# Expert stages in two arms with tighter capacities, their order written out for five engines

## The chip, the core and the metric

The kernel runs on one core of one Trainium2 chip. A core has TensorE (matmuls, with the load of the stationary operand shown as PEld), VectorE (DVE), ScalarE (ACT), GpSimd (POOL) and SyncE (SP), which here issues most of the DMAs. Each engine has its own instruction queue, and they wait for each other by semaphores. The metric is the device time of one execution in microseconds; lower is better.

## The reference, cut to what matters

```python
attn_out = _attn_ref(q, k, v, n_global, n_local)      # 2 batches, 8 heads, 768 x 64, a local window and global columns
x = attn_out.transpose(0, 2, 1, 3).reshape(1536, 512)
x = _moe_ref(x, w_in, w_out)                          # h = x @ w_in; g = h * tanh(softplus(h)); g @ w_out
# routed experts, N, D, E, F = 1536, 512, 8, 1024
logits = x @ w_gate
expert_idx = argmax(logits, axis=1)
for e in range(E):
    mask = expert_idx == e
    h = maximum(x[mask] @ w1[e], 0)
    out[mask] = gate_w[mask, None] * (h @ w2[e])
```

Each token goes to the one expert of its largest logit. How many tokens an expert gets is known only when the kernel runs.

## The kernel before, in words

The kernel has three parts. Attention and the dense layer take about the first 365 us. They write the tokens that leave the dense layer to a buffer `xg` in DRAM, each behind the others of its expert, by an indirect DMA. Then `final_rank` orders the experts by their number of tokens, and the rest of the kernel works through them from the fullest to the emptiest. This third part is what the change touches.

The work of the third part is cut into nine stages, listed in `STG`. A stage is a rank, an offset and a fixed number of token columns, its capacity: stage 0 has the first 160 tokens of the fullest expert (`EARLY`), stage 1 the rest of its capacity of 336, so 176, and stages 2 to 8 have one expert each with the capacities 288, 256, 224, 208, 200, 184 and 176 (`CAPS`). Columns behind the last token of an expert hold zeros and an invalid row number. If an expert has more tokens than the capacity of its rank, a flag makes a slow path behind the stages run.

A stage has eight steps m. In step m, `b_L1(g, m)` multiplies the tokens by 128 columns of the first weight matrix, in four accumulating matmul groups; two steps later (`LAG`) `b_L2(g, m)` multiplies the result by 128 rows of the second, into four accumulators `bacc`. float32 values are split into a high and a low part in the fp32r format, and three products are summed (`mm3`). Below 256 columns the high and the low part of the tokens lie side by side and one matmul of twice the width does two of the products (`cat`): a pair of matmuls a group. From 256 columns on it is three matmuls. So a stage has 64 pairs or 64 triples: 32 in `b_L1`, 32 in `b_L2`.

The other engines work beside these matmuls:

- The weights of the next expert come in eight loads of 512 KB (`b_raw`, on SyncE's queue, six buffers). Each is split in two halves by a cast on ScalarE (L160) and a subtraction on VectorE (L161): 16 casts and 16 subtractions an expert (`b_conv`).
- The result of a `b_L1` of fewer than 256 columns is copied by ScalarE (L768), added by VectorE (L769), activated by ScalarE (L776), and VectorE makes its low part (L777). From 256 columns on only the last two are there.
- The token rows of the next stage are loaded (`b_xload`), transposed on TensorE 128 at a time (L721), and split by ScalarE (L726) and VectorE (L727), in `b_xprep`, at step 5.
- When a stage's last `b_L2` is done, `b_yevac` takes the four accumulators out (ScalarE L809, VectorE L810); then `b_yout` transposes them back (L824), scales them (L826, VectorE) and scatters them to the output by GpSimd (L828), 128 tokens at a time.

The order of the first part is written out by hand. The order in each engine's queue in the third part is a scheduler's, which goes by the order of the program text and by its own estimate of when things are ready, over all stages and the early one at once. At the very end each engine loads a flag (L1148) and branches over the slow path (L1149).

Of the kernel before, what the change touches and what calls it, by code (L numbers as in the profile page):

```python
# [8 lines left out]
F32 = mybir.dt.float32  # L9
# [23 lines left out]
CAPS = [336, 288, 256, 224, 208, 200, 184, 176]  # L33
CAPMAX = max(CAPS)
# [9 lines left out]
def moe_kernel(ctx, tc, q, k, v, n_global, n_local, w_in, w_out, w_gate, w1, w2, out, dbg=None):  # L44
# [608 lines left out]
    STG = [(0, 0, EARLY), (0, EARLY, CAPS[0] - EARLY)] + [(r, 0, CAPS[r]) for r in range(1, NE)]  # L653
# [8 lines left out]
    braw = {}  # L662
    bx = {}
# [6 lines left out]
    def b_raw(r, i):  # L670
        which, f, kk = CH[i]
        er = ereg[r]
        if r == 0:
            if kk == 0:
                w0f[which, f] = wp.tile([128, 4, 512], F32, tag="w", name="w0f")
            st = w0f[which, f][:, 2 * kk:2 * kk + 2, :]
        else:
            st = stp.tile([128, 2, 512], F32, tag="st", name="bst")
# [6 lines left out]
    def b_conv(r, i):  # L685
        which, f, kk = CH[i]
        if kk == 0:
            pool, tag = (wp, "w") if nsw[0] % 6 != 3 else (wlate[0], "w2")
            nsw[0] += 1
            sw[r, which, f] = [pool.tile([128, 4, 512], F32R, tag=tag, name="bw") for _ in range(2)]  # L690
# [6 lines left out]
    def b_xload(g):  # L697
# [3 lines left out]
        for i in range(nt):  # L701
            n = min(128, cap - i * 128)
            xr = xe.tile([128, ROW], F32, tag="x2", name="xr")
# [8 lines left out]
    def b_xprep(g):  # L712
        cap = STG[g][2]
        bp = bpool[0]
        meta = bp.tile([128, 3, 2], F32, tag="meta", name="meta", bufs=4)
        idi = bp.tile([128, 3], I32, tag="idi", name="idi", bufs=4)
        xc = bp.tile([128, 4, 2, cap] if g else [128, 4, cap], F32R if g else F32, tag="xc", name="xc")
        for i, (xr, n) in enumerate(bx[g]):
            tp = ps.tile([128, 4, 128], F32, tag="b", name="btp")
# [10 lines left out]
        bx[g] = (meta, idi, xc)  # L730
# [14 lines left out]
    def b_L1(g, m):  # L745
# [3 lines left out]
        hp = ps.tile([128, 512], F32, tag="b", name="bhp")  # L749
# [8 lines left out]
        wh, wl = sw[r, 1, m // 4]  # L758
        cs = slice((m % 4) * 128, (m % 4) * 128 + 128)
        for kk in range(4):  # L760
            mm3(hp, cap, cat, wh[:, kk, cs], wl[:, kk, cs], xc[:, kk, 0, :], xc[:, kk, 1, :],
                xc[:, kk].rearrange("p a c -> p (a c)"), kk == 0, kk == 3)
        if cat:
            hc = wk.tile([128, 2, cap], F32R, tag="gh", name="hc", bufs=3)
            hh, hl = hc[:, 0], hc[:, 1]
            hc = hc.rearrange("p a c -> p (a c)")
            t1 = wk.tile([128, cap], F32, tag="e", name="t1")
            nc.scalar.copy(t1, hp[:, cap:2 * cap])  # L768
            nc.vector.tensor_add(t1, t1, hp[:, 0:cap])  # L769
            src = t1  # L770
        else:
            hc = None
            hh = wk.tile([128, cap], F32R, tag="gh", name="hh", bufs=3)
            hl = wk.tile([128, cap], F32R, tag="gl", name="hl", bufs=3)
            src = hp[:, 0:cap]
        nc.scalar.activation(out=hh, in_=src, func=AF.Relu)  # L776
        ins = nc.vector.scalar_tensor_tensor(out=hl, in0=src, scalar=0.0, in1=hh.bitcast(F32),  # L777
                                             op0=ALU.max, op1=ALU.subtract)
        if g == 1:
            hlast[m] = ins.ins  # L780
        hcs[g, m] = (hh, hl, hc)

    def b_L2(g, m):
        r, _, cap = STG[g]
        cat = cap < 256
        if m == 0:
            bacc[g] = [ps.tile([128, 512], F32, tag="b", name="bacc") for _ in range(4)]
# [12 lines left out]
    yss = {}  # L800

    def b_yevac(g):
        cap = STG[g][2]
        acc = bacc.pop(g)
        yss[g] = [wk.tile([128, cap], F32, tag="n" if d < 2 else "r", name="ys") for d in range(4)]
        for d in range(4):
            ys = yss[g][d]
# [8 lines left out]
    def b_yout(g):  # L816
        cap = STG[g][2]
        meta, idi, _ = bx.pop(g)
        ys = yss.pop(g)
        for i in range((cap + 127) // 128):  # L820
            n = min(128, cap - i * 128)
            tp = ps.tile([128, 512], F32, tag="b", name="ytp")
            for d in range(4):
                nc.tensor.transpose(tp[0:n, d * 128:(d + 1) * 128], ys[d][:, i * 128:i * 128 + n], ident)  # L824
            yo = wk.tile([128, DM], F32, tag="cv", name="yo")
            nc.vector.tensor_scalar(out=yo[0:n], in0=tp[0:n, :], scalar1=meta[0:n, i, 1:2], scalar2=None,  # L826
                                    op0=ALU.mult)
# [145 lines left out]
    bpool[0] = main.enter_context(tc.tile_pool(name="bp", bufs=2, side="right"))  # L973
# [70 lines left out]
    def final_rank():  # L1044
# [16 lines left out]
        capr = const.tile([1, NE], F32, name="capr")  # L1061
        for r in range(NE):
            nc.gpsimd.memset(capr[:, r:r + 1], float(CAPS[r]))
# [7 lines left out]
        flagf = const.tile([1, 2], F32, name="flagf")  # L1071
# [4 lines left out]
        flag = const.tile([1, 2], I32, name="flag")  # L1076
# [9 lines left out]
    def early_block():  # L1086
# [19 lines left out]
        b_yevac(0)  # L1106

    early_block()
    for i in range(8, NM + YLAG + 1):
        g, m = divmod(i, 8)  # L1110
        if i < NM:
            r = STG[g][0]
            b_L1(g, m)
            if m == 0 and g > 1 and g + 1 < len(STG):
                b_reg(r + 1)
            if m == 0 and g + 1 < len(STG):
                b_xload(g + 1)
            if m == 5 and g + 1 < len(STG):
                b_xprep(g + 1)
# [241 lines left out]
```

## Time and profile before

| | us |
|---|---|
| median of 3 runs | 578.6 |
| lowest and highest of them | 577.35 to 579.09 |
| profiled execution, its own time | 578.08 |
| its span, first to last instruction | 576.4 |

The profiled execution is 0.1% below the median. The span is what the trace covers; the execution's own time has 1.7 us around it. The granted TensorE clock is 0.996 of full speed over the span. Engines run side by side, so their busy times don't add up to the span.

### The profile page before, as it was taken

The numbers are of one execution on the slowest core, as the hardware profiler recorded it, in microseconds if no ns is written. First come the engines' busy times: TensorE is split into PE (matmuls) and PEld (weight loads), VectorE is DVE, ScalarE is ACT, GpSimd is POOL, SyncE is SP. The second block draws the span as 40 slices with busy tenths as digits, with TensorE's granted clock in tenths as the row PEclk, the third lists the DMA queues.
The fourth block names the chain that finished last, engine by engine and source line by source line (L and its number), as shares of the span: only waits on it lengthen the run. The fifth ranks groups of instructions, "written<-read, shape, count | busy, mean of one in ns | idle before, by whom it ended". The sixth has DMA issues, their size and how long they took to land.

```text
span 576.4 us, 12667 instructions
## 1 busy us (share of the span) xinstructions
PE 560.0 (97%) x4650; PEld 517.7 (90%) x4650; DVE 470.0 (82%) x1142; ACT 379.6 (66%) x890; POOL 82.6 (14%) x155
## 2 busy tenths in 40 slices
PE   8999999999999999999999999899999999999993
PEld 6898989988999898989898988699999999999993
DVE  7899999899999997687776868486966687988842
ACT  7999899795767676456565555366645466777631
POOL 3113010010000100101011111041121211211111
PEclk9999999999999999999999999999999999999998
DMA  8969699697877453423423211947837457478100
GB/s 249 275 218 353 175 341 329 182 341 242 279 233 252 140 187 98 145 78 107 146 90 113 92 38 38 326 158 264 278 128 288 148 218 266 165 264 288 62 19 22
DMA packets 54653, 110.00 MB, mean 191 GB/s; under 512 B 5439, under 2 KB 12607, under 8 KB 54582
## 3 DMA queue, kind: packets, MB, share of 16 engines
q1 hardware_dynamic: 48882, 90.21, 46.9%
q0 software_dynamic: 5696, 18.89, 9.7%
q8 instruction: 38, 0.62, 0.4%
q14 instruction: 33, 0.27, 0.1%
q10 hardware_dynamic: 4, 0.00, 0.0%
HBM read 84.67 MB, written 25.10 MB: 190 GB/s over the span
## 4 chain that ended last, share of the span: by engine, by line
PE 85%; DVE 7%; DMA 2%; ACT 2%; issue 2%; SPq 1%; POOL 0%; DVEq 0%; POOLq 0%; ACTq 0%
PE hp L437 24%; PE acc L456 21%; PE bacc L734 6%; PE bhp L734 6%; PE av L374 3%; PE sp L308 3%; PE bacc L735 3%; PE bhp L735 3%; DVE bw L161 2%; PE pt L344 1%; PE bhp L737 1%; PE bacc L737 1%; PE pt L346 1%; PE bacc L739 1%; PE bacc L738 1%
## 5 line engine op out<-in xcount | busy, mean ns | idle before, releaser
L456 PE MATMUL acc<-wpair,gh 128*128 128x512 f32 x384 | 120.9, 396 | 1.4 <-ACT gh L493 1.4
L437 PE MATMUL hp<-xh,wpair 128*128 128x256 f32 x768 | 118.5, 286 | 0.0
L437 PEld LDWEIGHTS hp<-xh,wpair 128*128 128x128 f32 x768 | 103.9, 188 | 3.6 <-ACT P L332 0.3
L161 DVE TENSOR_TENSOR bw<-bst,bw 128x512 fp32r<-128x512 f32 x112 | 72.9, 686 | 10.4 <-ACT bw L160 9.9
L456 PEld LDWEIGHTS acc<-wpair,gh 128*128 128x128 f32 x384 | 68.1, 188 | 13.7 <-ACT gh L493 1.9
L160 ACT CAST bw<-bst 128x512 fp32r<-128x512 f32 x112 | 64.3, 620 | 19.8 <-PE bhp L738 9.7
L456 PE MATMUL acc<-wpair,gl 128*128 128x512 f32 x192 | 75.3, 394 | 0.0
L464 ACT ACTIVATE e<-hp 128x512 f32<-128x512 f32 x48 | 28.7, 599 | 51.0 <-PE hp L437 50.8
L437 PE MATMUL hp<-xl,wpair 128*128 128x256 f32 x384 | 62.0, 283 | 0.0
L734 PE MATMUL bhp<-xc,bw 128*128 128x352 f32 (+4 forms) x192 | 59.3, 364 | 0.7 <-DVE t L769 0.6
L734 PE MATMUL bacc<-hc,bw 128*128 128x352 f32 (+4 forms) x192 | 59.2, 364 | 0.0
L437 PEld LDWEIGHTS hp<-xl,wpair 128*128 128x128 f32 x384 | 52.3, 188 | 0.6 <-issue 0.3
L735 PE MATMUL bhp<-xc,bw 128*128 128x176 f32 (+4 forms) x192 | 48.5, 253 | 0.0
L735 PE MATMUL bacc<-hc,bw 128*128 128x176 f32 (+4 forms) x192 | 48.3, 252 | 0.0
L332 ACT ACTIVATE P<-P,mx 128x232 f32<-128x232 f32 (+1 forms) x96 | 44.7, 472 | 1.6 <-DVE mx L321 1.5
L456 PEld LDWEIGHTS acc<-wpair,gl 128*128 128x128 f32 x192 | 36.0, 188 | 8.4 <-DVE gl L496 0.6
L474 DVE SCALAR_TENSOR_TENSOR n<-n,r 128x512 f32<-128x512 f32 x48 | 33.3, 693 | 11.4 <-ACT r L472 10.8
L493 ACT ACTIVATE gh<-n 128x512 fp32r<-128x512 f32 x48 | 30.1, 626 | 16.1 <-DVE n L489 16.1
L468 ACT ACTIVATE n<-e 128x512 f32<-128x512 f32 x48 | 30.3, 632 | 12.2 <-DVE e L466 12.0
L734 PEld LDWEIGHTS bhp<-xc,bw 128*128 128x128 f32 x192 | 36.1, 188 | 1.7 <-DVE t L769 0.8
L496 DVE SCALAR_TENSOR_TENSOR gl<-n,gh 128x512 fp32r<-128x512 f32 x48 | 32.9, 686 | 5.3 <-ACT gh L493 4.3
L735 PEld LDWEIGHTS bhp<-xc,bw 128*128 128x128 f32 x192 | 36.7, 191 | 0.0
(191 smaller groups left out, 1226.5 us busy)
## 6 DMA issues: line engine op xcount, KB each, us to landing
bst<-in_moe_w_dram SPq DMA_DIRECT2D x56, 512.0 KB
wst<-in_moe_w_in_dram SPq DMA_DIRECT2D x16, 512.0 KB
wst<-in_moe_w_out_dram SPq DMA_DIRECT2D x16, 512.0 KB
xps<-xpo SPq DMA_DIRECT2D x24, 256.0 KB
xh<-xs POOLq DMA_DIRECT2D x12, 512.0 KB, 4.9
xl<-xs POOLq DMA_DIRECT2D x12, 512.0 KB, 4.2
xpl<-xps SPq DMA_DIRECT2D x24, 256.0 KB
xg<-z SPq DMA_DIRECT2D x24, 224.9 KB
```

The lines of the kernel that those rows point to most:

```text
L160: nc.scalar.copy(hi, src)
L161: nc.vector.tensor_sub(lo, src, hi.bitcast(F32))
L332: nc.scalar.activation(out=Ps[s][:, q_, 0:w], in_=Ps[s][:, q_, 0:w], func=AF.Exp, bias=mxs[s][:, q_:q_ + 1], scale=-1.0, accum_out=rcs[t][ ...
L437: yield lambda f=f, kk=kk, wi=wi, xx=xx, cs=cs: nc.tensor.matmul(hp[:, f, :], lhsT=w[:, wi, kk, cs], rhs=xx[:, kk, :], start=(kk == 0 and ...
L456: yield lambda f=f, o=o, cs=cs, gi=gi, wi=wi, first=first, last=last: nc.tensor.matmul(accs[b][o], lhsT=gi[:, cs], rhs=w[:, wi, f, :], sta ...
L464: nc.scalar.activation(out=e, in_=hp, func=AF.Exp, scale=-1.0)
L468: nc.scalar.activation(out=n, in_=e, func=AF.Square)
L474: nc.vector.scalar_tensor_tensor(out=n, in0=n, scalar=0.25, in1=r, op0=ALU.add, op1=ALU.mult)
L493: nc.scalar.mul(gts[u][0], n, -(2.0 ** -80))
L496: nc.vector.scalar_tensor_tensor(out=gl, in0=n, scalar=-(2.0 ** -80), in1=gh.bitcast(F32), op0=ALU.mult, op1=ALU.subtract)
L734: nc.tensor.matmul(o[:, 0:2 * cap], lhsT=wh, rhs=xc, start=first, stop=False)
L735: nc.tensor.matmul(o[:, 0:cap], lhsT=wl, rhs=xh, start=False, stop=last)
```

## The change

The third part behind stage 0 is put into a function `rest()`, which is written into the program twice: once with the stages of a new list of capacities, `TIGHT`, and once with those of `CAPS`. A third flag tells whether an expert has more tokens than `TIGHT` allows its rank; the first arm runs when none has. Stage 1 of the first arm has 288 - 160 = 128 columns. Within an arm the order of each of the five engines is that of the program text (`manual_schedule`): in a step below 256 columns ScalarE copies, casts one half of a weight load, activates and casts the other half; VectorE adds, subtracts, makes the low part and subtracts. Then come the load of the sixth-next weight buffer, the transposes of a tile of tokens (one tile a step at steps 5 to 7), `b_L2`, at step 1 `b_yevac`, and at steps 2 to 4 one tile of `b_yout`, whose odd tiles ScalarE scales. The buffers are rings that are used in turn: twelve for weights, six for their loads, four PSUM banks for accumulators and four for everything else in PSUM. The six expert numbers and the two flags are loaded ahead of the arms.

```diff
+TIGHT = [288, 264, 232, 216, 200, 184, 176, 160]
...
-    STG = [(0, 0, EARLY), (0, EARLY, CAPS[0] - EARLY)] + [(r, 0, CAPS[r]) for r in range(1, NE)]
+    def stages(caps):
+        return [(0, 0, EARLY), (0, EARLY, caps[0] - EARLY)] + [(r, 0, caps[r]) for r in range(1, NE)]
+
+    STG = stages(CAPS)
+    ring = {}
+    rpos = {}
...
+    def buf(kind, pool, shape, dtype, tag, name, **kw):
+        if kind not in ring:
+            return pool.tile(shape, dtype, tag=tag, name=name, **kw)
+        i = rpos[kind]
+        rpos[kind] = (i + 1) % len(ring[kind])
+        return shaped(ring[kind][i], shape, dtype)
...
-    def b_xprep(g):
+    def b_xprep(g, only=None):
...
+        for i, (xr, n) in enumerate(rows):
+            if only is not None and i != only:
+                continue
...
-    def b_L1(g, m):
+    def b_L1(g, m, part=None):
...
+        if part == 0:
+            wh, wl = sw[r, 1, m // 4]
+            cs = slice((m % 4) * 128, (m % 4) * 128 + 128)
+            for kk in range(4):
+                mm3(hp, cap, cat, wh[:, kk, cs], wl[:, kk, cs], xc[:, kk, 0, 0:cap], xc[:, kk, 1, 0:cap],
+                    xc[:, kk, :, 0:cap], kk == 0, kk == 3)
+            src = hp[:, 0:cap]
+            if cat:
+                src = buf("e", wk, [128, cap], F32, "e", "t1")
+                nc.scalar.copy(src, hp[:, cap:2 * cap])
+                nc.vector.tensor_add(src, src, hp[:, 0:cap])
+            hps_b[g, m] = hp, src
+            return
...
         nc.scalar.activation(out=hh, in_=src, func=AF.Relu)
-        ins = nc.vector.scalar_tensor_tensor(out=hl, in0=src, scalar=0.0, in1=hh.bitcast(F32),
-                                             op0=ALU.max, op1=ALU.subtract)
-        if g == 1:
-            hlast[m] = ins.ins
+        nc.vector.scalar_tensor_tensor(out=hl, in0=src, scalar=0.0, in1=hh.bitcast(F32),
+                                       op0=ALU.max, op1=ALU.subtract)
...
-    def b_yout(g):
+    def b_yout(g, i):
...
+        if i % 2:
+            nc.scalar.mul(yo[0:n], tp[0:n, :], meta[0:n, i, 1:2])
+        else:
             nc.vector.tensor_scalar(out=yo[0:n], in0=tp[0:n, :], scalar1=meta[0:n, i, 1:2], scalar2=None,
                                     op0=ALU.mult)
...
+        for r in range(NE):
+            nc.gpsimd.memset(capr2[:, r:r + 1], float(TIGHT[r]))
+        nc.vector.tensor_tensor(out=over, in0=rank.unsqueeze(2).to_broadcast([1, NE, NE]),
+                                in1=io8[0:1, :].unsqueeze(1).to_broadcast([1, NE, NE]), op=ALU.is_equal)
+        nc.vector.tensor_tensor(out=over, in0=over, in1=capr2.unsqueeze(1).to_broadcast([1, NE, NE]), op=ALU.mult)
+        lim2 = const.tile([1, NE], F32, name="lim2")
+        nc.vector.reduce_sum(out=lim2, in_=over, axis=AX.X)
+        nc.vector.tensor_tensor(out=lim2, in0=cnt, in1=lim2, op=ALU.is_gt)
+        flagf = const.tile([1, 3], F32, name="flagf")
+        nc.vector.reduce_max(out=flagf[:, 2:3], in_=lim2, axis=AX.X)
...
     early_block()
-    for i in range(8, NM + YLAG + 1):
-        g, m = divmod(i, 8)
-        if i < NM:
-            r = STG[g][0]
-            b_L1(g, m)
...
+    ring["w"] = [flat(wp.tile([128, 4, 512], F32R, tag="w", name="bw"), 2048) for _ in range(4)]
+    ring["w"] += [flat(t, 2048) for k_ in ((0, 1, 0), (0, 2, 0), (0, 1, 1), (0, 2, 1)) for t in sw[k_]]
+    ring["st"] = [flat(t, 1024) for t in raw1]
...
+    banks = [flat(ps.tile([128, 512], F32, tag="b", name="bank"), 512) for _ in range(8)]
+    ring["acc"], ring["hp"] = banks[0:4], banks[4:8]
...
+    def rest():
+        convs = [(r, n) for r in range(1, NE) for n in range(8)]
+        todo = []
+
+        def cast(r, n, k2):
+            which, f, kk = CH[n]
+            if kk == 0 and k2 == 0:
+                sw[r, which, f] = [buf("w", wp, [128, 4, 512], F32R, "w", "bw") for _ in range(2)]
+            hi, lo = sw[r, which, f]
+            st, kx = braw[r, n][:, k2, :], 2 * kk + k2
+            nc.scalar.copy(hi[:, kx, :], st)
+            subs.append((lo[:, kx, :], st, hi[:, kx, :].bitcast(F32)))
+
+        subs = []
+
+        def sub():
+            if subs:
+                nc.vector.tensor_sub(*subs.pop(0))
+
+        for i in range(8, NM + YLAG + 1):
+            g, m = divmod(i, 8)
+            n = i - 10
+            conv = 0 <= n < len(convs)
+            if i < NM:
+                b_L1(g, m, 0)
+                if STG[g][2] >= 256:
+                    sub()
+                    b_L1(g, m, 1)
+                    if conv:
+                        cast(*convs[n], 0)
+                else:
+                    if conv:
+                        cast(*convs[n], 0)
+                    if len(subs) > 1 or not conv:
+                        sub()
+                    b_L1(g, m, 1)
+                sub()
+                if conv:
+                    cast(*convs[n], 1)
+            else:
+                sub()
+            if 1 <= n and n + 5 < len(convs):
+                b_raw(*convs[n + 5])
+            if m == 1 and g + 1 < len(STG):
+                b_xload(g + 1)
+            if m >= 5 and g + 1 < len(STG):
+                b_xprep(g + 1, m - 5)
+            if i - LAG >= 8 and i - LAG < NM:
+                g2, m2 = divmod(i - LAG, 8)
+                b_L2(g2, m2)
+                if m2 == 7:
+                    b_yevac(g2)
+            if i >= 10 and m >= 2 and (m < 5 or g == len(STG)):
+                todo.append((g - 1, m - 2))
+            while todo:
+                g2, t = todo.pop(0)
+                last = b_yout(g2, t)
+                if last and g2 == len(STG) - 3:
+                    nc.gpsimd.drain()
...
+    for r in range(2, NE):
+        b_reg(r)
+    loose = nc.values_load(flag[0:1, 2:3], min_val=0, max_val=1)
+    slow = nc.values_load(flag[0:1, 0:1], min_val=0, max_val=1)
+    before = [dict(d) for d in state]
+    STG[:] = stages(TIGHT)
+    hand = {mybir.EngineType.PE, mybir.EngineType.Activation, mybir.EngineType.DVE, mybir.EngineType.Pool, mybir.EngineType.SP}
+    with tc.If(loose < 1) as cmp:
+        with tc.manual_schedule(engines=hand):
+            rest()
+    for d, o in zip(state, before):
+        d.clear()
+        d.update(o)
+    STG[:] = stages(CAPS)
+    with cmp.Else():
+        with tc.manual_schedule(engines=hand):
+            rest()
...
-    slow = nc.values_load(flag[0:1, 0:1], min_val=0, max_val=1)
     with tc.If(slow > 0):
```

## Rows read from the trace of the kernel before

**Rows 1.** The page: busy us and share of the span, all engines.

```profile
PE 560.0 (97%) x4650; PEld 517.7 (90%) x4650; DVE 470.0 (82%) x1142; ACT 379.6 (66%) x890; POOL 82.6 (14%) x155
```

**Rows 2.** Windows by stage: length, then busy us of each engine, clock, DMA.

```profile
392.40:410.87 18.47, 17.88 (x133) 17.38 (x133) 15.46 (x35) 11.33 (x30) 3.98 (x12) 1.00 0.71 237
...
526.01:545.82 19.81, 19.81 (x147) 19.59 (x145) 18.02 (x41) 14.22 (x39) 2.52 (x2) 1.00 0.50 179
...
sum 174.00, PE 173.41 PEld 170.85 DVE 132.34 ACT 105.09 POOL 28.68; mean PE 21.68 PEld 21.36 DVE 16.54 ACT 13.14 POOL 3.58
```

**Rows 3.** Timeline of TensorE: start, length; pairs of 176, 224, triples 256, 288.

```profile
394.11 0.35 PE L734 MATMUL bhp<-xc,bw 128*128 128x352 f32 x1
...
395.20 0.35 PE L734 MATMUL bhp<-xc,bw 128*128 128x352 f32 x1
...
480.28 0.38 PE L734 MATMUL bacc<-hc,bw 128*128 128x448 f32 x1
...
482.18 0.38 PE L734 MATMUL bhp<-xc,bw 128*128 128x448 f32 x1
...
451.27 0.28 PE L737 MATMUL bacc<-hh,bw 128*128 128x256 f32 x1
...
453.75 0.28 PE L737 MATMUL bhp<-xc,bw 128*128 128x256 f32 x1
...
424.25 0.30 PE L737 MATMUL bhp<-xc,bw 128*128 128x288 f32 x1
...
427.81 0.29 PE L737 MATMUL bhp<-xc,bw 128*128 128x288 f32 x1
```

**Rows 4.** Groups by line and shape behind 392 us: busy, mean ns.

```profile
L161 DVE TENSOR_TENSOR bw<-bst,bw 128x512 fp32r<-128x512 f32 x112 | 72.9, 686 | 10.4 <-ACT bw L160 9.9
L160 ACT CAST bw<-bst 128x512 fp32r<-128x512 f32 x108 | 62.1, 620 | 15.0 <-PE bhp L738 9.7 <-PE bacc L738 1.7 <-DMA bst<-in_moe_w_dram 1.7
...
L776 ACT ACTIVATE hc<-t 128x200 fp32r<-128x200 f32 x8 | 3.0, 371 | 5.0 <-DVE t L769 5.0
...
L769 DVE TENSOR_TENSOR t<-t,bhp 128x200 f32<-128x200 f32 x8 | 2.8, 353 | 0.0
...
L777 DVE SCALAR_TENSOR_TENSOR hc<-t,hc 128x200 fp32r<-128x200 f32 x8 | 2.9, 363 | 1.5 <-ACT hc L776 1.5
```

**Rows 5.** Timeline around the end of the early stage.

```profile
388.28 1.14 ACT L160 CAST bw<-bst 128x512 fp32r<-128x512 f32 x2 [4.77 <-DMA bst<-in_moe_w_dram]
...
389.68 2.61 PE L791 MATMUL bacc<-hf,w0f 128*128 128x160 f32 x16 [1.01 <-ACT hf L755]
...
391.39 0.95 DVE L727 TENSOR_TENSOR xc<-btp,xc 128x512 fp32r<-128x512 f32 x2 [4.83 <-ACT xc L726]
...
393.77 0.31 ACT L768 COPY t<-bhp 128x176 f32<-128x176 f32 x1 [1.15 <-PE bhp L735]
```

**Rows 6.** Timeline of the kernel's end.

```profile
565.67 1.13 ACT L809 COPY ys<-bacc 128x176 f32<-128x176 f32 x4 [1.33 <-PE bacc L735]
...
566.01 1.16 DVE L810 TENSOR_TENSOR ys<-ys,bacc 128x176 f32<-128x176 f32 x4 [1.29 <-ACT ys L809]
...
569.23 1.00 POOL L828 DMA_INDIRECT out_dram<-yo,idi  x1 [10.04 <-DVE yo L826]
...
570.53 0.91 POOL L828 DMA_INDIRECT out_dram<-yo,idi  x1 [0.30 <-issue]
```

**Rows 7.** The instructions of line 1148, the load of the branch's flag.

```profile
L1148 PEldq TENSOR_LOAD <-flag x1: 486/486/486, 567.2 to 567.2; - x1
...
L1148 POOLq TENSOR_LOAD <-flag x1: 503/503/503, 569.7 to 569.7; - x1
```

**Rows 8.** The instructions of line 1149, the branch at the kernel's end.

```profile
L1149 PEldq COMPARE_BRANCH  x1: 3338/3338/3338, 567.8 to 567.8; - x1
...
L1149 POOLq COMPARE_BRANCH  x1: 58/58/58, 570.3 to 570.3; - x1
...
L1149 POOLq EVENT_SEMAPHORE  x6: 17/30/43, 573.5 to 574.4; - x6
```

More of the change, by code (lines that the diff above doesn't have):

```diff
@@ L662, in moe_kernel @@
     braw = {}
+    raw1 = []
     bx = {}
@@ L677, in b_raw @@
         else:
-            st = stp.tile([128, 2, 512], F32, tag="st", name="bst")
+            st = buf("st", stp, [128, 2, 512], F32, "st", "bst")
+            if "st" not in ring:
+                raw1.append(st)
         if which == 1:
@@ L689, in b_conv @@
             nsw[0] += 1
-            sw[r, which, f] = [pool.tile([128, 4, 512], F32R, tag=tag, name="bw") for _ in range(2)]
+            sw[r, which, f] = [buf("w", pool, [128, 4, 512], F32R, tag, "bw") for _ in range(2)]
         hi, lo = sw[r, which, f]
@@ L786, in b_L2 @@
         if m == 0:
-            bacc[g] = [ps.tile([128, 512], F32, tag="b", name="bacc") for _ in range(4)]
+            bacc[g] = [buf("acc", ps, [128, 512], F32, "b", "bacc") for _ in range(4)]
         if g == 0:
@@ L804, in b_yevac @@
         acc = bacc.pop(g)
-        yss[g] = [wk.tile([128, cap], F32, tag="n" if d < 2 else "r", name="ys") for d in range(4)]
+        yss[g] = [buf("ys", wk, [128, cap if g else 512], F32, "n" if d < 2 else "r", "ys") for d in range(4)]
         for d in range(4):
-            ys = yss[g][d]
+            ys = yss[g][d][:, 0:cap]
             if g and cap < 256:
@@ L1061, in final_rank @@
         capr = const.tile([1, NE], F32, name="capr")
+        capr2 = const.tile([1, NE], F32, name="capr2")
         for r in range(NE):
@@ L1075, in final_rank @@
         nc.vector.tensor_max(flagf[:, 0:1], flagf[:, 0:1], flagf[:, 1:2])
-        flag = const.tile([1, 2], I32, name="flag")
+        flag = const.tile([1, 3], I32, name="flag")
         flagt[0] = flag
@@ new lines, in moe_kernel @@
+    flag = flagt[0]
+    ring["ys"] = [flat(t, 512) for t in ys0]
+    ring["w"] = [flat(wp.tile([128, 4, 512], F32R, tag="w", name="bw"), 2048) for _ in range(4)]
+    ring["w"] += [flat(t, 2048) for k_ in ((0, 1, 0), (0, 2, 0), (0, 1, 1), (0, 2, 1)) for t in sw[k_]]
+    ring["st"] = [flat(t, 1024) for t in raw1]
+    ring["x2"] = [flat(xe.tile([128, ROW], F32, tag="x2", name="xr"), ROW) for _ in range(3)] + [flat(xr3, ROW)]
+    for tag, n in (("gh", 3), ("gl", 3), ("e", 2), ("cv", 2)):
+        ring[tag] = [flat(wk.tile([128, 512], F32R if tag[0] == "g" else F32, tag=tag, name=tag, **({"bufs": 3} if n == 3 else {})), 512) for _ in range(n)]
```

135 lines of the change are left out of this document (68 added, 67 removed).

## The prediction

> **What bounds the kernel now.** I read the page first: TensorE works 560.0 of 576.4 us [rows 1]. Then the windows cut at the first matmul of each expert stage: from 392.40 to 566.40 us TensorE is busy for 173.41 of 174.00 us at a granted clock of 1.00 [rows 2]. The only idle time is in the first of these stages (18.47 long, 17.88 busy). So this stretch is as long as its matmuls, and the change, which lies behind 380 us, is worth what it takes out of TensorE's queue, unless another queue takes over. VectorE is the candidate: 18.02 of 19.81 us in the stage of 184 columns [rows 2].
>
> Third, the timeline of TensorE gives the price of columns. A stage makes 64 steps of two matmuls (below 256 columns) or of three. From start to start four pairs of 176 columns take 395.20 - 394.11 = 1.09, so 0.273 each; six of 224 take 1.90, so 0.317; seven triples of 256 take 2.48, so 0.354; nine of 288 take 3.56, so 0.396 [rows 3]. A pair so costs 0.92 ns a column more, a triple 1.3 ns. Check: 64 pairs of 184 at 0.280 are 17.9 us, and with 16 transposes the stage has 19.81, so 0.11 a transpose.
>
> **Fewer columns.** By these prices the stages behind the early one cost 64 x (0.273 + 0.396 + 0.354 + 0.317 + 0.302 + 0.295 + 0.280 + 0.273) = 159.3 us. The tight arm has 128, 264, 232, 216, 200, 184, 176 and 160 columns: 64 x (0.23 + 0.365 + 0.324 + 0.309 + 0.295 + 0.280 + 0.273 + 0.258) = 149.3. All but 128 and 160 lie between measured widths; at 128 the pair may cost from 0.22 (two transposes' pace) to 0.273 (no gain below 176), and I take the line. The stage of 128 writes one tile of tokens and not two, four transposes less: 0.4 us. With the 0.6 us of idle time TensorE's own gain is 10.0 + 0.4 + 0.6 = 11.0 us. The arm is the tight one where the counts allow it: the reference on its default inputs gives 269, 258, 202, 196, 190, 182, 124 and 115 tokens, each under its capacity.
>
> **VectorE in the stage of 128 columns.** TensorE needs 56 pairs and 20 transposes there, 56 x 0.23 + 20 x 0.11 = 15.1 us. VectorE must, in the order written, do 8 additions and 8 residuals (0.353 and 0.363 at 200 columns [rows 4], some 0.29 at 128), 12 weight residuals at 72.9/112 = 0.65, one output tile and three token tiles: 4.6 + 7.8 + 0.7 + 1.5 = 14.6. It starts 1.4 us late (first block, copy) and idles about 1.1 in the two steps that have no weights yet, so the last token residual ends near 17.1, and the next stage's first matmul reads it. Cost 2.0 us; from 0 (hidden) to 3.3 (18.47 as before).
>
> **The accumulators between stages.** At step 1 of a stage the order now puts both weight casts ahead of the evacuation of the previous stage, and at step 2 TensorE needs its accumulators back. For 200 columns, from the end of the step's first-layer block: a block of four pairs is 1.18, so TensorE wants the first accumulator at 2.36. ScalarE starts its copy 0.2 after a block's end (393.77 against 394.11 - 2 x 0.27 = 393.57 [rows 3, 5]), copies until 0.5 (four such took 1.13 [rows 6]), casts (62.1/108 = 0.57) until 1.07, activates (0.37) until 1.44, casts until 2.0, then copies accumulators, 0.27 apart [rows 4, 6]. VectorE meanwhile adds, subtracts, makes the residual behind the activation (until 1.9) and subtracts again until 2.55; its first accumulator is done at 2.85. TensorE waits 0.5 us; the other three follow 0.28 apart [rows 6], its own pace. The wait is 0.35 at 232 columns and 0.85 at 160, in six stages some 3.5 us. Below: 0, if ScalarE reaches the copies a cast earlier. Above: 1.4 each, 8.3 us, if it must wait for the fourth accumulator.
>
> **The order ahead of the arms.** Before, a cast of the next expert's weights stood in ScalarE's queue ahead of two activations of the early stage and waited 4.77 us for its DMA; TensorE waited 1.01 us for the activation behind it [rows 5]. The cast now lies inside the arm, so the activations, the tokens' cast behind them and the first matmul at 392.40 come 1.0 us earlier. From -1.0 to 0.
>
> **Entering the arm.** Each engine loads two flags (0.49 us each on TensorE [rows 7]) and branches. TensorE's loads lie beside the early stage's last 16 matmuls (2.6 us [rows 5]), the others' beside TensorE's first block; uncovered they would cost 1.0. SyncE's six expert numbers stood at the same place before. I take 0: the tight arm is written first, and the branch falls through into it. The trace shows no branch that isn't taken; the nearest rows, taken ones, lose 3.3 us on TensorE [rows 8], and that is the upper end.
>
> **Leaving it.** Every engine now jumps over the other arm and then takes the jump that was there. GpSimd's is at 570.3, and its next instruction comes at 573.5 [rows 8]: 3.2 us, which were hidden behind the last scatter, issued until 571.44 [rows 6]. With two in a row, and the flag's load (0.5 [rows 7]) gone: 569.8 + 3.2 + 3.2 = 576.2 against 574.4, when its last wait ended before [rows 8]: 1.8 us later. If the semaphores' levelling at the end of the arm holds the first jump until the scatter is issued, 4.1. I take 3.0, less 0.2 because ScalarE now scales the second output tile beside VectorE: 2.8. TensorE's two jumps, 3.3 each from 567.3 on [rows 8], end near 574, under that. [...]
>
> **No cost.** Weight loads are issued when a buffer's last residual is done, half a step after the last cast from it and four and a half ahead of the next, some 10 us; a stage's eight loads of 512 KB were moved before too in 19.81 us, at 179 GB/s [rows 2]. On SyncE the token rows stand behind one such load, four steps ahead of use; if a load came late, ScalarE's cast would wait, and behind it the activations that TensorE needs two steps later. The eight capacities (GpSimd) and five more tiny operations on VectorE push its last weight residuals into the 4.83 us for which it idles before 391.39 [rows 5].
>
> **Sum.** -11.0 + 2.0 + 3.5 - 1.0 + 0 + 2.8 = -3.7 us on the profiled execution's 578.08 (its span is 576.4; the rest lies outside): 574.4. The median of the runs is 578.6, 0.5 above, so I say 574.5, 0.7% faster. A change of 0.3%, 1.7 us, is about what a measurement of this kernel can tell from none.
>
> **Rivals.**
> - No waits: ScalarE and VectorE keep up, at the boundaries and in the stage of 128. For it: both are below TensorE's time in every stage. Against: the queues above. 578.1 - 11.0 - 1.0 + 1.8 = 567.9, or 570.6 with half of the 5.5 us of waits. Chance 0.17.
> - [...] Chance 0.11. [...]
> - VectorE becomes the bound, slower than before: in the stages of 216 to 176 columns its fixed order makes it wait for ScalarE inside each step. Its work is some 17.3 us (18.02 in the stage of 184, less an output tile of 0.7, now ScalarE's) against TensorE's 19 to 21.5, and it hands over to ScalarE twice in a step. Each 0.1 us by which a step outlasts TensorE's is 3.2 us in these four stages; from 0.17 a step on (5.5 us) the kernel is slower, and with 0.25 it takes 574.5 + 8 = 582. For it: 91% busy in the stage of 184. Against: in that stage TensorE never waited [rows 2]. Chance 0.13.
> - The former arm runs: the columns stay, 578.1 - 1.0 + 2.8 + 2 at the boundaries = 582. Against: the counts. Chance 0.04.
>
> **How the numbers follow.** The forecast has 0.55; its own range, from the bounds of boundaries and exit, is 572 to 577. Faster: 0.51 of it, the 0.17 and 0.02 of the entry's, 0.70. Same: 0.04 + 0.09 + 0.02 = 0.15. Slower: 0.11 + 0.04 = 0.15. The range leaves a tenth at each end: 569 to 580.
>
> **What would show it.** Right: pairs 0.26 to 0.33 us apart in the new widths; TensorE idle for 0.3 to 0.9 us before the first accumulating matmul of each stage, released by VectorE's addition of the evacuation; 2 us of idle ahead of the stage of 264 columns, released by the token residual; the early stage ending near 391.3; last wait of GpSimd some 3 us further behind the last scatter than now. Wrong: no such idle (then 568 to 571), a gap of 3 us on all engines near 391, or VectorE at 97% with TensorE waiting in every step.

## The result: 1.2% faster, and the profile after

Four runs of the changed kernel gave a median of 571.01 us (570.07 to 572.11), four of the kernel before 578.15. The ratio is 0.9877, with a 95% interval of 0.985 to 0.9903. The forecast was 574.5 with a range of 569 to 580: the sign and the range held, the gain was under-estimated. The profiled execution after took 570.47 us with a span of 568.7; the one before 578.08 and 576.4. That is 7.6 us, where the sum of the prediction had 3.7.

The windows of the kernel before, cut anew at the first matmul of the early stage, the first matmul of the stage behind it and the last stage's last matmul (columns as in [rows 2]):

```profile
370.73:392.40 21.67, 20.55 (x176) 19.45 (x174) 14.14 (x49) 14.21 (x37) 5.88 (x6) 1.00 0.66 232
392.40:566.46 174.06, 173.47 (x1281) 170.91 (x1281) 132.40 (x284) 105.15 (x263) 28.68 (x47) 1.00 0.54 191
566.46:576.36 9.90, 1.25 (x8) 0.72 (x8) 2.11 (x5) 0.34 (x2) 1.90 (x2) 0.78 0.10 32
```

The same windows of the kernel after; the second is followed by its eight stages, of 128, 264, 232, 216, 200, 184, 176 and 160 columns:

```profile
370.58:390.61 20.03, 20.03 (x175) 19.38 (x174) 14.95 (x54) 12.19 (x32) 6.05 (x6) 1.00 0.60 210
...
390.61:557.00 166.39, 164.40 (x1216) 159.68 (x1214) 127.08 (x285) 111.16 (x285) 25.80 (x46) 1.00 0.64 202
...
390.61:406.15 15.54, 15.20 (x135) 14.92 (x133) 12.46 (x31) 12.16 (x34) 3.46 (x8) 1.00 0.77 252
406.15:430.23 24.08, 23.90 (x196) 23.69 (x197) 16.61 (x33) 12.68 (x30) 2.37 (x5) 1.00 0.71 224
430.23:453.54 23.31, 23.21 (x159) 21.64 (x157) 17.53 (x37) 15.39 (x37) 4.41 (x7) 1.00 0.67 213
453.54:475.37 21.83, 21.64 (x147) 20.73 (x145) 17.81 (x40) 15.86 (x40) 2.96 (x6) 1.00 0.74 225
475.37:496.60 21.23, 20.99 (x147) 20.45 (x145) 17.44 (x40) 15.40 (x40) 3.59 (x6) 1.00 0.76 239
496.60:516.92 20.32, 20.05 (x146) 19.62 (x145) 17.11 (x40) 15.04 (x40) 3.81 (x6) 1.00 0.73 239
516.92:536.78 19.86, 19.55 (x147) 19.14 (x145) 16.82 (x40) 14.85 (x40) 2.15 (x2) 1.00 0.70 216
536.78:557.00 20.22, 19.86 (x155) 19.49 (x153) 11.30 (x31) 9.78 (x30) 3.04 (x6) 1.00 0.04 14
557.00:568.68 11.68, 1.51 (x9) 0.83 (x8) 1.43 (x4) 1.01 (x3) 1.86 (x2) 0.74 0.13 34
```

So the balance is: ahead of the early stage -0.15, early stage -1.64, stages -7.67, behind the last matmul +1.78; sum -7.68. The page after, as [rows 1]: every engine but ScalarE does less, and the bound is TensorE as before.

```profile
PE 550.7 (97%) x4582; PEld 507.3 (89%) x4582; DVE 465.3 (82%) x1148; ACT 384.3 (68%) x908; POOL 78.8 (14%) x162
```

In 2.0 us of the stages TensorE is not busy (166.39 against 164.40), where it was 0.6 before. Who is waited for there is told by the waits, first of TensorE's matmuls, then of its weight loads (us in total, times, longest):

```profile
PE bank L777 <- DVE ys L860: 1.4, 5, 0.4
...
PEld bank L777 <- DVE ys L860: 2.5, 5, 0.6
PEld bank L780 <- ACT xc L768: 0.5, 1, 0.5
PEld bank L781 <- DVE xc L769: 0.4, 1, 0.4
PEld bank L777 <- issue: 0.4, 1, 0.4
```

These are the two waits that the prediction named: the accumulators at step 2 of a stage (six places: five released by L860, and one that shows as "issue"), and the tokens of the stage of 264 columns. The weight loads' rows are the ones to read. At the boundary below, the weight load stops for 0.48 us while the matmul ahead of it is still running, so that the matmuls' row shows 0.24; and what the stages lose there is the weight loads' 2.9 us (2.85, see e4), not the matmuls' 1.4.

How such a boundary looks, in the timelines of ScalarE, VectorE, matmuls and weight loads where the stage of 200 columns takes over from that of 216:

```profile
480.25 0.60 ACT L1207 CAST bw<-bst 128x512 fp32r<-128x512 f32 x1
480.75 1.05 ACT L859 COPY ys<-bank 128x216 f32<-128x216 f32 x4
...
480.73 0.68 DVE L1214 TENSOR_TENSOR bw<-bst,bw 128x512 fp32r<-128x512 f32 x1
481.33 1.24 DVE L860 TENSOR_TENSOR ys<-ys,bank 128x216 f32<-128x216 f32 x4
...
481.76 0.45 PE L777 MATMUL bank<-gh,bw 128*128 128x400 f32 x1 [0.24 <-DVE ys L860]
...
481.76 0.19 PEld L777 LDWEIGHTS bank<-gh,bw 128*128 128x128 f32 x1 [0.48 <-DVE ys L860]
```

The second cast (480.25) and the second subtraction (480.73) stand ahead of the evacuation, as forecast, and TensorE's weight load waits 0.48 us for the first addition. But each instruction starts before the one ahead of it has ended: the cast of 0.60 us gives way after 0.50, the subtraction of 0.68 after 0.60.

### The profile page after: what moved, and what is told of

Its sections match the earlier page's. It is cut to its first block, busy times and chain, and to the rows that moved or that the text cites. A ratio compares the mean times of both kernels' runs of the same rounds, so it can differ in the third digit from the quotient of the medians.

```text
span 568.7 us, 12525 instructions
## 1 busy us (share of the span) xinstructions
PE 550.7 (97%) x4582; PEld 507.3 (89%) x4582; DVE 465.3 (82%) x1148; ACT 384.3 (68%) x908; POOL 78.8 (14%) x162
## 4 chain that ended last, share of the span: by engine, by line
PE 87%; DVE 8%; issue 1%; DMA 1%; POOL 1%; ACT 1%; SPq 0%; POOLq 0%; ACTq 0%; DVEq 0%
PE hp L438 24%; PE acc L457 21%; PE bank L777 14%; PE bank L778 6%; PE sp L309 3%; PE av L375 3%; PE bhp L801 2%; PE bacc L840 2%; DVE bw L1214 1%; PE pt L345 1%; PE bank L875 1%; PE pt L347 1%; PE bank L781 1%; PE bank L780 1%; PE bank L782 1%
## 5 line engine op out<-in xcount | busy, mean ns | idle before, releaser
L1214 DVE TENSOR_TENSOR bw<-bst,bw 128x512 fp32r<-128x512 f32 x112 | 76.5, 685 | 0.5
L777 PE MATMUL bank<-gh,bw 128*128 128x256 f32 (+6 forms) x224 | 68.2, 363 | 1.5 <-DVE ys L860 1.4
L1207 ACT CAST bw<-bst 128x512 fp32r<-128x512 f32 x112 | 68.3, 617 | 0.0
L777 PE MATMUL bank<-xc,bw 128*128 128x256 f32 (+6 forms) x224 | 67.9, 361 | 0.0
L778 PE MATMUL bank<-xc,bw 128*128 128x128 f32 (+6 forms) x224 | 55.5, 248 | 0.0
L778 PE MATMUL bank<-gh,bw 128*128 128x128 f32 (+6 forms) x224 | 55.5, 248 | 0.0
L777 PEld LDWEIGHTS bank<-gh,bw 128*128 128x128 f32 x224 | 42.1, 188 | 3.9 <-DVE ys L860 2.5
L777 PEld LDWEIGHTS bank<-xc,bw 128*128 128x128 f32 x224 | 42.1, 188 | 1.0
L815 ACT COPY e<-bank 128x128 f32<-128x128 f32 (+6 forms) x56 | 17.7, 317 | 37.2 <-PE bank L778 36.6
L778 PEld LDWEIGHTS bank<-xc,bw 128*128 128x128 f32 x224 | 42.8, 191 | 0.0
L778 PEld LDWEIGHTS bank<-gh,bw 128*128 128x128 f32 x224 | 42.8, 191 | 0.0
```

The costliest lines, as they stand in the source:

```text
L777: nc.tensor.matmul(o[:, 0:2 * cap], lhsT=wh, rhs=xc, start=first, stop=False)
L778: nc.tensor.matmul(o[:, 0:cap], lhsT=wl, rhs=xh, start=False, stop=last)
L815: nc.scalar.copy(src, hp[:, cap:2 * cap])
L1207: nc.scalar.copy(hi[:, kx, :], st)
L1214: nc.vector.tensor_sub(*subs.pop(0))
```

## The experiments

Medians, ratios with intervals, and three stretches of each profiled execution, from windows cut as above. The start of the early stage, 370.6 to 374.2 us in these traces, wanders by itself and is left out.

| kernel | us | ratio to before | early stage | stages | behind last matmul |
|---|---|---|---|---|---|
| before | 578.15 | 1 | 21.67 | 174.06 | 9.90 |
| after | 571.01 | 0.9877 (0.985 to 0.9903) | 20.03 | 166.39 | 11.68 |
| e1 columns alone | 569.63 | 0.9857 (0.9832 to 0.9882) | 20.93 | 165.83 | 9.24 |
| e2 order alone | 581.48 | 1.0052 (1.0032 to 1.0073) | 20.04 | 176.44 | 11.86 |
| e3 one arm | 569.69 | 0.9843 (0.9818 to 0.9868) | 20.03 | 166.50 | 9.80 |
| e4 evacuation first | 568.18 | 0.9824 (0.9802 to 0.9845) | 20.03 | 163.56 | 11.79 |
| e5 arms swapped | 579.57 | 1.0036 (1.0022 to 1.005) | 24.88 | 171.18 | 10.05 |
| e6 casts back | 573.20 | 0.9923 (0.991 to 0.9937) | 21.05 | 166.52 | 11.88 |
| e7 preparation early | 571.04 | 0.9873 (0.9858 to 0.9888) | 20.04 | 165.41 | 11.69 |
| e8 one arm, e4, e7 | 565.90 | 0.9782 (0.9768 to 0.9795) | 20.03 | 162.58 | 9.23 |
| e9 e8 without branches | 562.95 | 0.9742 (0.9727 to 0.9757) | 20.04 | 162.57 | 7.34 |
| e10 two arms, e4, e7 | 567.92 | 0.983 (0.9804 to 0.9856) | 20.04 | 162.56 | 11.54 |

The kernel before ran beside each batch with medians of 578.88 (e1 to e4) and 578.09 (e5 to e10); the ratios are to these. The last stretch comes from one execution each and wanders: 9.23 to 10.05 us with one jump at the end, 11.54 to 11.88 with two.

**e1: the columns alone, in the kernel before.**

```
-CAPS = [336, 288, 256, 224, 208, 200, 184, 176]
-CAPMAX = max(CAPS)
+CAPS = [288, 264, 232, 216, 200, 184, 176, 160]
+CAPMAX = 336
```

> The kernel before with the list of capacities replaced by the tight one and nothing else (old order, one path; a fuller expert would go to the fallback). Theory A, columns alone are worth what the prediction's term says: 578.15 - 11.0 = 567.1 us, with the sum of the stages near 163. Rival B, the old order loses at the narrow stages too (accumulators, VectorE in the stage of 128 columns): 569 to 571 us, sum of the stages 166 or more. The stretch from the start of the early stage to the first matmul of the next stage stays at 21.67 us by A and by B.

Rival B by the time; the sum of its stages, 165.83, falls just short of B's 166. The columns alone take the time to 569.6: no worse than the whole change. But the old order loses where the stages get narrow. Its stage of 128 columns, then the waits of its matmuls over all stages:

```profile
391.90:408.65 16.75, 15.48 (x134) 15.03 (x133) 14.13 (x33) 10.65 (x29) 4.53 (x12) 1.00 0.75 251
...
PE bhp L734 <- DVE t L769: 1.0, 2, 0.6
```

The stage takes 16.75 us, and TensorE waits for VectorE's additions. The early stage is 0.7 us shorter too, which neither theory had. Of this 0.5 us is a DMA: the weights that ScalarE's cast waits for are there 17.03 us after the stage's start, not 17.55. The rest goes with its last preparation, which at a capacity of 288 has one tile of tokens instead of two (its cast takes 0.58 us instead of 0.80, its subtraction 0.69 instead of 0.95). The changed kernel does not get this rest, since it prepares the first stage at the former capacity ahead of the branch.

**e2: the order, rings and arms alone, at the former capacities.**

```
-    STG[:] = stages(TIGHT)
+    STG[:] = stages(CAPS)
     hand = ...
     with tc.If(loose < 1) as cmp:
```

> The changed kernel with the former capacities in both arms: the order, the rings and the arms alone, no fewer columns. Theory A (terms as read from the trace after): early stretch -1.6, tail +1.8, accumulators between the stages +1.3, so 578.15 + 1.5 = 579.7 us (578.8 to 580.5). Rival B, the written order is itself part of the gain: 576.5 us or less. Rival C, the accumulators cost what the prediction said (3.5): 581.9 us.

Above A's span, at C's edge: the order and the arms alone make the kernel 0.5% slower. The three stretches give -1.63, +2.38 and +1.96, in all +2.7, against a measured ratio that is +3.0 us of 578.88. A was too low because I had taken its +1.3 for the accumulators from the matmuls' waits; the weight loads of this run wait 2.3 us there, and 0.9 us more for the tokens of the second stage (L780, L781), which A had left out:

```profile
PEld bank L777 <- DVE ys L860: 2.0, 4, 0.5
...
PEld bank L777 <- issue: 0.3, 1, 0.3
```

**e3: the tight arm alone.**

```
+        nc.vector.tensor_max(flagf[:, 0:1], flagf[:, 0:1], flagf[:, 2:3])
...
-    with tc.If(loose < 1) as cmp:
-        with tc.manual_schedule(engines=hand):
-            rest()
...
-    with cmp.Else():
-        with tc.manual_schedule(engines=hand):
-            rest()
+    with tc.manual_schedule(engines=hand):
+        rest()
```

> The changed kernel with the tight arm alone, no If and no second arm; the fallback's flag also covers a tight capacity that is exceeded, so the former arm is left out. Theory A, the arm costs the second jump at the end alone: tail 9.9 instead of 11.68 us, early stretch unchanged, 571.0 - 1.8 = 569.2 us. Rival B, the early stretch was shortened by the arm's edge, which keeps the weight cast of the next stage out of it: without the arm the cast comes back ahead of the last activation, early stretch +1.6, 570.8 us. Rival C, the end waits for something else than the jump: 571.0 us.

Theory A: 569.7, stretch behind the last matmul 9.80 instead of 11.68, and the early stage still 20.03. The former arm's price is 1.9 us between these two traces, all of it at the end. The early stage does not need the arm to be shorter: the hand-written order keeps the next expert's casts behind it, with or without a branch.

**e4: one move in the order.** Step 1 of a stage evacuates the former accumulators ahead of the second cast and subtraction.

```
+                if m == 1 and g > 1:
+                    b_L2(g - 1, 7)
+                    b_yevac(g - 1)
                 sub()
                 if conv:
                     cast(*convs[n], 1)
...
-            if i - LAG >= 8 and i - LAG < NM:
+            if 8 <= i - LAG < NM and (m != 1 or i >= NM):
```

> The changed kernel with one move: in step 1 of a stage the evacuation of the former stage's accumulators stands ahead of the second weight cast and its subtraction on ScalarE and VectorE. Theory A, those two instructions make the first bank of the next stage late: the waits for a bank at L777 (1.5 us of TensorE in all) go, 571.0 - 1.4 = 569.6 us. Rival B, the chain of copies and additions itself sets the bank's release: the waits stay, 570.7 to 571.0 us. Rival C, the subtraction that is now late delays the next relu chain: waits of the same size appear at the next step's matmuls, 571.0 us.

The mechanism of A, with twice its size: 568.2 us. The six stages lose no time at all any more, and every wait for L860 is gone from the list. Two of its windows, for 200 and 160 columns:

```profile
475.56:496.30 20.74, 20.74 (x146) 20.44 (x145) 17.34 (x40) 15.44 (x40) 4.28 (x6) 1.00 0.75 240
...
535.43:555.07 19.64, 19.64 (x155) 19.46 (x153) 11.18 (x31) 9.80 (x30) 2.90 (x6) 1.00 0.04 14
```

Against the same stages after, the six are shorter by 0.34, 0.39, 0.49, 0.50, 0.55 and 0.58: 2.85 us. The delayed subtraction harms nothing.

**e5: the arms exchanged**, so that the arm that runs is jumped to and then needs no jump at its end.

```
-    STG[:] = stages(TIGHT)
+    STG[:] = stages(CAPS)
...
-    with tc.If(loose < 1) as cmp:
+    with tc.If(loose > 0) as cmp:
...
-    STG[:] = stages(CAPS)
+    STG[:] = stages(TIGHT)
     with cmp.Else():
```

> The changed kernel with its arms exchanged: the former capacities under If, the tight ones under Else, so that the tight arm is jumped to and ends without a jump. [...] Rival B, the jump is only dear at the end, and at the entry other work hides it: 569.1 us. [...]

B falls: 579.6 us, slower than the kernel before. At the end the jump's price is saved (10.05 instead of 11.68), but nothing hides the entry, which costs far more than the 3.3 us that the prediction had as its upper end. The branch as TensorE's queue shows it, the weight loads behind it (the last column is idle time), and windows of these microseconds:

```profile
L1267 PEldq COMPARE_BRANCH  x1: 6237/6237/6237, 389.5 to 389.5; - x1
...
395.88 0.29 PEld L777 LDWEIGHTS bank<-xc,bw 128*128 128x128 f32 x1 [4.79 <-issue]
...
399.52 0.29 PEld L778 LDWEIGHTS bank<-xc,bw 128*128 128x128 f32 x1 [2.07 <-issue]
...
394.00:395.00 1.00, 0.00 (x0) 0.00 (x0) 0.00 (x0) 0.00 (x0) 0.00 (x0) 0.50 0.57 201
395.91:397.50 1.59, 1.51 (x6) 1.54 (x7) 0.00 (x0) 0.00 (x0) 0.00 (x0) 0.50 0.11 28
...
403.50:405.50 2.00, 2.00 (x19) 2.00 (x18) 1.25 (x4) 1.50 (x4) 0.00 (x0) 0.94 0.00 0
```

The jump takes 6.24 us on TensorE, seven weight loads later its queue stops once more for 2.07 without waiting for anyone, and the granted clock, which had been 1.00, falls to 0.50 while TensorE stands in the first stop of 4.6 us. It is 0.50 from 394 us on, and on the mean 0.94 between 403.5 and 405.5, with TensorE at work from 399.5 on. The early stage's stretch grows by 4.85 and the stage of 128 columns, now 20.29, by 4.75. What the jump waits for in its 6.24 us, no row shows; the second stop and the clock are told by this run alone. In the changed kernel the same branch is not taken and costs 0.086 us (at 389.1; the 3.438 of the same line is the jump at the arm's end):

```profile
L1267 PEldq COMPARE_BRANCH  x2: 86/1762/3438, 389.1 to 557.7; - x2
```

**e6: the casts back ahead of the early stage's last two relus** (their result is not used).

```
+        for i in (0, 1):
+            for k2 in range(2):
+                scr = wk.tile([128, 512], F32R, tag="cv", name="scr")
+                with tc.high_priority():
+                    nc.scalar.copy(scr, braw[1, i][:, k2, :])
         for m in range(8 - LAG, 8):
```

> The changed kernel with four weight casts put back on ScalarE ahead of the last two relus of the early stage, two and two as in the kernel before; their result is not used. Theory A, both waits of the early stage's last matmuls return: the stretch from its start to the next stage's first matmul goes from 20.04 to 21.6 us, 571.0 + 1.6 = 572.6 us. Rival B, only the one wait of 1.0 us that the prediction counted: 572.0 us. Rival C, the stretch is shorter because the arms' code starts with a written order, not because of the casts: 571.0 us, stretch 20.04.

C falls: 573.2 us, and the casts lengthen the early stage. The size is B's (+1.02 in the stretch) by the mechanism of A. ScalarE's first cast and TensorE's weight loads:

```profile
387.80 1.14 ACT L1181 CAST scr<-bst 128x512 fp32r<-128x512 f32 x2 [4.18 <-DMA bst<-in_moe_w_dram]
...
389.19 1.11 PEld L840 LDWEIGHTS bacc<-hf,w0f 128*128 128x128 f32 x8 [0.54 <-ACT hf L803]
390.60 1.11 PEld L840 LDWEIGHTS bacc<-hf,w0f 128*128 128x128 f32 x8 [0.30 <-ACT hf L803]
```

The first cast waits for its DMA, which here landed 16.96 us after the early stage's start and in the kernel before 17.55 [rows 5]: 0.6 us earlier, which is as much as this run's stretch lacks to 21.67. The second pair of casts holds up the second relu in the same way, with 0.30 us of waiting for it. The median is 2.2 us above that of the kernel after; 1.0 of it stands in this stretch, and the rest in none that the edit touches.

**e7: the three tiles of the 264 columns' tokens prepared one step earlier.**

```
-            if m >= 5 and g + 1 < len(STG):
-                b_xprep(g + 1, m - 5)
+            if g + 1 < len(STG):
+                x0 = 4 if g == 1 else 5
+                if x0 <= m < x0 + 3:
+                    b_xprep(g + 1, m - x0)
```

> The changed kernel with the preparation of the rows of the stage of 264 columns (three tiles) one step earlier in the stage of 128. Theory A, the half microsecond that TensorE waits for xc at the start of the stage of 264 (0.34 and 0.18, and some behind the weight loads) goes: 571.0 - 0.5 = 570.5 us. Rival B, VectorE in the stage of 128 columns has no room for it earlier and the wait moves into that stage: 571.0 us or more, with new waits between 400 and 406 us.

The time, 571.04, cannot tell 0.5 us from none. The windows can: the two stages take 15.04 and 23.61 us instead of 15.54 and 24.08, without a wait, so 0.97 went (A, with twice its size: both ends of the wait, in this stage and in the one behind). This execution reached its early stage 1.8 us later than the one after did, ahead of anything that the move touches.

```profile
392.41:407.45 15.04, 15.04 (x134) 14.90 (x134) 11.65 (x30) 11.34 (x32) 3.67 (x8) 1.00 0.73 240
407.45:431.06 23.61, 23.61 (x199) 23.61 (x198) 17.43 (x34) 13.53 (x33) 2.38 (x5) 1.00 0.78 235
```

**e8: one arm and both moves.** The edits of e3, e4 and e7.

> One arm, the evacuation first and the earlier preparation together; the former arm is left out, and the fallback covers an exceeded tight capacity. Theory A, the three gains stand in different stretches and add: 571.0 - 1.9 (tail) - 2.8 (accumulators) - 0.5 (first boundary) = 565.8 us, stages 163.1, tail 9.8. Rival B, a gain of one is taken back by another: 567 us or more, and then the stage table shows where.

A: 565.9 us, stages 162.58 and 9.23 behind them. The gains stand in different stretches and add. With a ratio of 0.9782 to the kernel before it beats both kernels; an expert above its tight capacity would go straight to the fallback.

**e9: e8 without the fallback's branch.**

```
-    slow = nc.values_load(flag[0:1, 0:1], min_val=0, max_val=1)
...
-    with tc.If(slow > 0):
-        ...
```

> The one-arm kernel of the run before (evacuation first, earlier preparation) with no branch at all behind the stages: the fallback and the former arm are left out, which the data shown never enter. [...] Rival B, the landing of the last scatter sets the end: tail 9.2, 565.9 us. [...]

B falls: 562.95 us, and a stretch of 7.34 behind the last matmul instead of 9.23. One jump at the end, with the load of its flag and the semaphores that go with it, so costs 1.9 us (against e8's 9.23) to 2.5 (e3's 9.80), and two 4.2 to 4.5 (11.54 and 11.88, e10's and e6's): some 2 us each, where TensorE's branch lasts 3.3 (before) to 4.2 us (L1280 of the kernel after). This kernel leaves out what a fuller expert would need.

**e10: the changed kernel with both moves, both arms kept.** The edits of e4 and e7.

> The changed kernel, both arms and the fallback kept, with the two moves of order (evacuation first in step 1, preparation of the three tiles one step earlier). Theory A, the gains add: 571.0 - 2.8 - 0.5 = 567.7 us, stages 162.6, tail 11.7. Rival B, they overlap: 568.2 us or more, as the evacuation alone.

By the stretches A (162.56 and 11.54): nothing is lost when the moves are made together. The median, 567.92, lies between A and B's bounds, and is not told apart from e4's.

## Why the prediction held, and why it was too small

Every place was as forecast. Where a size was off, it was off in the same direction, towards too little gain, so that the errors added up to 3.8 us instead of cancelling. The mechanism of the exit was another one than forecast, and ahead of the arms there was more of it. The measured 571.0 lies below the 572 to 577 that the forecast had for itself, and inside 569 to 580, which is wider because of the rivals.

| term of the sum | forecast | measured | from |
|---|---|---|---|
| Fewer columns | -11.0 | -11.5 | 174.06 to 162.56, e10, whose stages have no wait |
| VectorE in the stage of 128 columns | +2.0 | +1.0 | after, 15.54 + 24.08, less e7's 15.04 + 23.61 |
| The accumulators between stages | +3.5 | +2.85 | after less e4, six stages |
| The order ahead of the arms | -1.0 | -1.64 | early stage, 21.67 to 20.03 |
| Entering the arm | 0 | 0 | branch not taken, 0.086 us on TensorE |
| Leaving it | +2.8 | +1.8 | 9.90 to 11.68; 1.9 by e3 |
| sum | -3.7 | -7.5 | and 0.15 ahead of the early stage |

**Fewer columns.** The pitches came out as read off the line, outside the measured widths too: two pairs of 128 columns start 0.23 apart in the kernel after.

```profile
390.90 0.34 PE L777 MATMUL bank<-xc,bw 128*128 128x256 f32 x1
...
391.13 0.33 PE L777 MATMUL bank<-xc,bw 128*128 128x256 f32 x1
```

Where the remaining 0.5 us lies is open. (By the prediction's own sum a transpose is 1.89/16 = 0.12 us, not 0.11, which is too little to matter here.)

**VectorE in the stage of 128 columns.** The cause was right, and the end of VectorE's work was put too late. I had it at 17.1 us into the stage; the last token residual ended at 406.67, 16.06 into it, where TensorE needed 15.04 (e7): 1.0 too late, not 2.0. VectorE's groups after, by line and shape (busy, mean ns), then its last token residual and the weight load that waits for it:

```profile
L1214 DVE TENSOR_TENSOR bw<-bst,bw 128x512 fp32r<-128x512 f32 x11 | 7.5, 684 | 0.0
L828 DVE SCALAR_TENSOR_TENSOR gh<-e,gh 128x128 fp32r<-128x128 f32 x8 | 2.3, 287 | 1.2 <-ACT gh L827 1.2
L816 DVE TENSOR_TENSOR e<-e,bank 128x128 f32<-128x128 f32 x8 | 2.3, 285 | 1.8 <-ACT e L815 1.7
L769 DVE TENSOR_TENSOR xc<-bank,xc 128x512 fp32r<-128x512 f32 x2 | 1.4, 692 | 0.0
...
406.49 0.18 DVE L769 TENSOR_TENSOR xc<-bank,xc 128x32 fp32r<-128x32 f32 x1
...
406.72 0.19 PEld L781 LDWEIGHTS bank<-xc,bw 128*128 128x128 f32 x1 [0.39 <-DVE xc L769]
```

With two single instructions of 0.7 and 0.3 the groups add up to 14.5, close to the 14.6 that I had counted, and yet the window shows VectorE busy for 12.46: neighbours overlap, 2.0 us over the window's 31 instructions. Against this VectorE stood idle for 1.9 us between its first addition and that residual, not 1.1. Ahead of the wait for the residual comes one of 0.48 us for ScalarE's cast of the same tokens (L768), which the forecast did not name. In e7 both are gone, though VectorE is busy as long over the two stages (29.08 us against 29.07): the work of the stage's last step no longer stands ahead of these two instructions.

**The accumulators between stages.** At 232 and 200 columns the wait is as forecast, 0.34 us for 0.35 and 0.49 for 0.5. The six together are 0.65 less, because the wait grows more slowly towards the narrow stages: at 160 columns it is 0.58, where the prediction has 0.85 without showing how.

**The order ahead of the arms.** I counted one wait, the 1.01 us of [rows 5], and let everything behind it come as much earlier. The weight loads show three stops. The first relu held them up for 1.14 us. The second pair of casts held up the second relu, which ended at 390.88, in the middle of the group of 16 weight loads, where the timeline folds it away: the group took 2.37 us, where it takes 2.20 in the kernel after. Behind that relu came ScalarE's cast of the tokens, and so the next stage's first weight load waited 0.35 us for their low part. In the kernel before:

```profile
389.67 2.37 PEld L791 LDWEIGHTS bacc<-hf,w0f 128*128 128x128 f32 x16 [1.14 <-ACT hf L755]
...
390.58 0.30 ACT L755 ACTIVATE hf<-bhp 128x160 f32<-128x160 f32 x1
...
392.40 0.19 PEld L734 LDWEIGHTS bhp<-xc,bw 128*128 128x128 f32 x1 [0.35 <-DVE xc L727]
```

From the stage's start to this group it is 18.94 us before and 17.86 after, from there to the next stage's first matmul 2.73 and 2.17: 1.08 + 0.56 = 1.64. e6 puts the casts back and loses 1.02 of it again, in both parts, so the casts are a cause; that the other 0.6 goes with the DMA that landed earlier there fits in size and is not shown by a run of its own.

**Leaving it.** The step that failed is GpSimd's 3.2 + 3.2, with the flag's load gone. Their sum, 1.8 us later than before, is what was measured, but by luck, since its parts came out otherwise; and the 1.2 us that I had added on top, for the case that the first jump is held up, was not paid. GpSimd's first jump, at 560.08, was nearly free: 0.48 us on, at 560.57, it loads the second flag (0.32 us). That load stands behind the jump on the chip, although the program's text has both flags ahead of the arms. The second branch starts at 560.96 and the next event comes at 566.3, 5.3 us later, while the last scatter ran from 560.97 to 561.85. The branch of line 1280 in the kernel after (ns; start):

```profile
L1280 POOLq EVENT_SEMAPHORE  x6: 17/30/43, 566.3 to 566.7; - x6
...
L1280 POOLq COMPARE_BRANCH  x1: 55/55/55, 561.0 to 561.0; - x1
L1280 PEldq COMPARE_BRANCH  x1: 4233/4233/4233, 561.9 to 561.9; - x1
...
L1280 POOLq INC_SWDGE_SEM  x1: 257/257/257, 566.8 to 566.8; - x1
```

GpSimd's queue sets the end, as forecast: from the start of that last instruction to the end of the span it is 1.9 us before (574.5 to 576.4), after (566.8 to 568.7), in e3 (565.3 to 567.2) and in e8 (564.1 to 566.0). VectorE's events come later, at 567.1, and TensorE's two jumps, 3.44 and 4.23 us, are done at 566.2; neither changes that distance. Why GpSimd's first jump was cheap and the second takes 5.3 us, where a single one takes 3.2 (before, e3 and e8), no run here tells. As the last stretch wanders, the second jump's price lies between 1.5 us (11.54 less 10.05) and 2.6 (11.88 less 9.23).

**The rivals.** "No waits" did not come true: 3.85 us of the forecast's 5.5 were paid. That the measured 571.0 lies next to its 570.6 is luck, for that sum has 2.75 us of waits, and the difference was made up by the columns and the early stage. The 0 for the entry was an estimate, since the trace before shows no branch that isn't taken; it held, with 0.086 us on TensorE. A stall there, with a chance of 0.11, was the right thing to fear, and its upper end of 3.3 us too low: where the arm is jumped to, in e5, the way in costs some 9.6 us (4.85 + 4.75). "VectorE becomes the bound" fell: in the stages of 216 to 176 columns TensorE waits at step 2 alone, and e4 leaves no wait. "The former arm runs" was priced at 582; e2, which runs the former capacities in that order, takes 581.5.

**What the change is worth.** All of the net gain is the columns', 8.3 us alone (e1, by its ratio: 1.4% of 578.88). Order and arms alone cost 3.0 (e2). In the stages the two together gain 1.8 us more than their sum (7.67 against 8.23 - 2.38), 1.2 of it in the stage of 128 columns, where the new order does better (15.54 against 16.75). With two instructions and one preparation moved, the order is what lets the narrow stages run without any wait of TensorE: 162.56 us against e1's 165.83.

## What to carry to other kernels

Where an order is written by hand, look at the step that gives a buffer back: what frees it belongs ahead of work that nobody waits for, here one cast and one subtraction, 2.85 us. When an engine's work is summed for a place in a queue, take start-to-start distances from the timeline (here 14.5 us of lengths were 12.46 of busy time), and for a stall of TensorE read the weight loads' waits (2.9 us here, where the matmuls' row has 1.4). Put the arm that runs where the branch falls through (8.6 us between e5 and the kernel after), and count the jumps behind the last matmul, some 2 us each here.

## What was not expected of the hardware

- A branch taken in mid-kernel (e5) cost TensorE 6.24 us, then 2.07 more seven weight loads on, and its granted clock, which fell during the first stop, was still 0.50 when it had worked again for 4 us (399.5 to 403.5); the jumps at the kernel's end took it 3.3 us before, 3.44 and 4.23 after. The branch that was not taken took 0.086 (after).
- Consecutive instructions of ScalarE and of VectorE overlap in the trace of the kernel after: a cast of 0.60 us is followed after 0.50, a subtraction of 0.68 after 0.60.
- Of GpSimd's two jumps in a row (after) the first cost under 0.5 us (0.48) and the second 5.3, where a single one takes 3.2 (before, e3, e8).
